# Whole-row weight pieces, a tile of its own for the last rows of v, and a conditional copy of x to DRAM

## The chip, the cores and the metric

The kernel runs on one core of one Trainium2 chip. The metric is device time in microseconds (us) of one execution, start to finish. Five engines work side by side, each in its own strict program order: PE (TensorE, matrix products), DVE (VectorE), ACT (ScalarE), POOL (GpSimd) and SP (SyncE). SP and POOL also issue most DMA transfers, and 16 DMA engines move the bytes for all of them.

## The reference

The first half is attention for 8 batches, 12 heads, 448 positions and head size 64, with an extra `exp(-m)` in the denominator. The second half is a mixture of experts over the 3584 resulting tokens of 768 numbers:

```
e   = exp(scores - m)
x   = (e / (sum(e) + exp(-m) + 1e-9)) @ v          # attention, then heads side by side: 3584 x 768
idx = argmax(cos(x, expert_emb) / tau)             # one of 8 experts for each token
out = gate * (relu(x @ w1[idx]) @ w2[idx])         # w1 768 x 1024, w2 1024 x 768 for each expert
```

With the inputs as drawn, all 448 tokens of a batch choose the same expert, in each of the 8 batches (worked out from the reference). The kernel doesn't rely on it: it runs each batch with the expert that most of its tokens chose, and a loop at the end (`other_experts`) handles the tokens that chose another one. For that loop x is kept in DRAM. With these inputs the loop has nothing to do.

## The kernel before, in words

**Tiling.** A *group* is two heads of one batch: 6 groups to a batch, 48 in all. Loads come for two groups at a time (24 loads, `n`). Of the 448 rows of q, k and v, 384 lie as 128 partitions x 3, and the last 64 rows, the *rest*, are handled apart. For a group, PE transposes q and k (`front_q`, `front_k`, L225 to L238), makes the scores in four pieces (L271, L281), ACT takes the exponential (L276), DVE subtracts 1 (L278), and PE multiplies with v (`attend`, L296, and `attend_rest`, L309). The tile `vab` holds v next to columns of ones, so that the same product also gives the denominator. POOL fills it from the loaded v (`front_v`, L249 to L257).

**Normalising.** For each two groups, the denominators go through a small DMA (`den`, L320) and DVE (`recip`, L336 to L340) to POOL, which makes the tile `rt` (L342). PE multiplies it by a selection matrix (`normalise`, L353), and DVE makes x from that (L358). Since 1 was subtracted, the sum of v over all positions is added back: POOL adds the four parts of v (`sum_v`, L194 to L196), DVE transposes and reduces it (`sum_v_rows`, L204 and L205). The tile `vs` has one buffer, so POOL's next sum can begin only when DVE's transpose has read the last one.

**Router and experts.** When a batch's six x are ready, PE, DVE and POOL find its expert (`router_mm` to `router_pick`). Then POOL issues the DMAs that fetch that expert's weights (`fetch`, L478), which also turn float32 into bfloat16. A batch's weights come in 8 pieces of 384 KB (as written): four of w1, each all 768 rows by 256 columns, and four of w2, each 256 rows by 768 columns. They share one pool of 10 buffers. `keep_xb` (L488) writes a batch's x, 672 KB, to DRAM. The expert's 15 pieces of work (`moe_chunks`: eight `h`, L495, then seven `y`, L510 and L525) are spread over six groups of later attention work.

**Order.** The work of all stages is laid out by hand in slots, 8 to a group (`pipeline`), and PE executes in just that order. For the other engines a scheduler places each instruction near its slot. A wait that is reached holds up everything behind it on that engine: a weight fetch on POOL stands in one line with `vs`, `vab` and `rt`, and on SP an output waits behind loads of q, k and v. Each `fetch` is also held behind the latest `front_v`. Outputs leave from three `y` buffers (L514 writes them on DVE, L548 and L554 issue the DMAs on SP), so the seventh `y` of a batch needs the buffer of the fourth.

**Rests of v.** `load_v` (L183 to L185) loads the main part, then the rests of all four heads into `vld` on partitions 0 to 63 (64 KB), and the rests of the odd heads a second time into the unused half of `qrest` on partitions 64 to 127 (32 KB), since `vab` needs them there (L257).

Of the kernel before, what the change touches and what calls it, by code (L numbers as in the profile page):

```python
# [9 lines left out]
F32 = mybir.dt.float32  # L10
F32R = mybir.dt.float32r
BF16 = mybir.dt.bfloat16
I32 = mybir.dt.int32
U32 = mybir.dt.uint32
ACT = mybir.ActivationFunctionType
ALU = mybir.AluOpType
# [21 lines left out]
def build_consts(k):  # L38
    nc, pool = k.nc, k.const
    k.ident = pool.tile([128, 128], F32, name="ident")  # L40
    make_identity(nc, k.ident[:])
    k.ones_f = pool.tile([128, 1], F32, name="ones_f")
    nc.vector.memset(k.ones_f[:], 1.0)
    iota_i = pool.tile([128, E], I32, name="iota_i")
    nc.gpsimd.iota(iota_i[:], pattern=[[1, E]], base=0, channel_multiplier=0)
    k.iota = pool.tile([128, E], F32, name="iota")
    nc.vector.tensor_copy(out=k.iota[:], in_=iota_i[:])

    k.vld, k.krest, k.qrest, k.vab, k.rc, k.vst = [], [], [], [], [], []
    for s in range(NG):  # L50
        v = pool.tile([128, 2 * GP, 4, DH], F32, name=f"vld{s}")
        nc.gpsimd.memset(v[64:128, :, 3, :], 0.0)
        k.vld.append(v)
        kr = pool.tile([128, GP, 128], F32, name=f"krest{s}")
        nc.vector.memset(kr[:], 0.0)
        k.krest.append(kr)
        qr = pool.tile([128, 2 * GP, DH], F32, name=f"qrest{s}")
        nc.gpsimd.memset(qr[64:128, GP:, :], 0.0)
        k.qrest.append(qr)
    for s in range(2):  # L60
        va = pool.tile([128, 4, 4, 64], F32R, name=f"vab{s}")
        for h in range(2):
            nc.vector.tensor_copy(
                out=va[:, :, 2 * h + 1, :],
                in_=k.ones_f[:, 0:1].unsqueeze(2).broadcast_to([128, 4, 64]),
            )
        k.vab.append(va)
        rc = pool.tile([128, CN], F32R, name=f"rc{s}")
        nc.vector.memset(rc[:].bitcast(F32), 0.0)
        k.rc.append(rc)  # L70
        k.vst.append(pool.tile([128, NG, 4 * GP], F32, name=f"vst{s}"))
# [50 lines left out]

def prep_expert_emb(k, emb_in, tau):
    nc = k.nc
    emb = k.wp.tile([E, DM], F32, name="emb_raw", tag="w")
    nc.sync.dma_start(emb[:], emb_in[:, :])
    sq = k.wp.tile([E, DM], F32, name="emb_sq", tag="w")
    ss = k.csp.tile([E, 1], F32, name="emb_ss", tag="cs")
    nc.scalar.activation(sq[:], emb[:], ACT.Square, accum_out=ss[:])
    nrm = k.csp.tile([E, 1], F32, name="emb_nrm", tag="cs")  # L130
    nc.gpsimd.tensor_tensor(out=nrm[:], in0=ss[:], in1=k.half[0:E, 0:1], op=ALU.pow)
    nc.vector.tensor_scalar_add(nrm[:], nrm[:], 1e-6)
    rs = k.csp.tile([E, 1], F32, name="emb_rs", tag="cs")
    nc.vector.reciprocal(out=rs[:], in_=nrm[:])
    nc.vector.tensor_scalar_mul(rs[:], rs[:], 1.0 / float(tau))
    ens = k.wp.tile([E, DM], F32, name="emb_scaled", tag="w")
    nc.vector.tensor_scalar_mul(ens[:], emb[:], rs[:])
    k.ens = ens

# [13 lines left out]
def load_qk(k, n):  # L153

    nc = k.nc
    b, h0 = n // NG, n % NG * 2 * GP
    g0, s = h0 // 2, n % NG
    t = Net()
    t.qm = k.qkp.tile([128, 3, 2 * GP, DH], F32, name="qm", tag="qm")
    t.km = k.qkp.tile([128, 3, 2 * GP, DH], F32, name="km", tag="km")  # L160
    t.kr, t.qr, t.v = k.krest[s], k.qrest[s], k.vld[s]

    def rest2(src, two):
        return src[b].rearrange("(g two) s d -> two s g d", two=2)[two, SM:S, g0 : g0 + GP, :]

    keng = nc.sync if n else nc.scalar
    for eng, dst, src in ((nc.sync, t.qm, k.q), (keng, t.km, k.k)):
        for j in range(3):
            eng.dma_start(
                dst[:, j, :, :], src[b, h0 : h0 + 2 * GP, 0:SM, :].rearrange("h (p t) d -> t p h d", t=3)[j]  # L170
            )
    nc.sync.dma_start(t.qr[0:64, :, :], k.q[b, h0 : h0 + 2 * GP, SM:S, :].rearrange("h p d -> p h d"))
    keng.dma_start(t.kr[0:64, :, 0:64], rest2(k.k, 0))
    keng.dma_start(t.kr[64:128, :, 64:128], rest2(k.k, 1))
    k.ld[n] = t


def load_v(k, n):

    nc, t = k.nc, k.ld[n]  # L180
    b, h0 = n // NG, n % NG * 2 * GP
    g0 = h0 // 2
    nc.sync.dma_start(t.v[:, :, 0:3, :], k.v[b, h0 : h0 + 2 * GP, 0:SM, :].rearrange("h (p t) d -> p h t d", t=3))  # L183
    nc.sync.dma_start(t.v[0:64, :, 3, :], k.v[b, h0 : h0 + 2 * GP, SM:S, :].rearrange("h p d -> p h d"))
    nc.sync.dma_start(  # L185
        t.qr[64:128, 0:GP, :], k.v[b].rearrange("(g two) s d -> two s g d", two=2)[1, SM:S, g0 : g0 + GP, :]
    )


def sum_v(k, n):  # L190

    nc, t = k.nc, k.ld[n]
    vs = k.vsp.tile([128, 2 * GP, DH], F32, name="vs", tag="vs")
    nc.gpsimd.tensor_tensor(out=vs[:], in0=t.v[:, :, 0, :], in1=t.v[:, :, 1, :], op=ALU.add)  # L194
    nc.gpsimd.tensor_tensor(out=vs[:], in0=vs[:], in1=t.v[:, :, 2, :], op=ALU.add)
    nc.gpsimd.tensor_tensor(out=vs[:], in0=vs[:], in1=t.v[:, :, 3, :], op=ALU.add)  # L196
    k.va[n] = vs


# [44 lines left out]
def front_v(k, g):  # L244
    nc = k.nc
    t, i = k.ld[g // GP], g % GP
    va = k.vab[g % 2]
    for h in range(2):
        nc.gpsimd.tensor_scalar(  # L249
            out=va[:, 0:3, 2 * h, :], in0=t.v[:, 2 * i + h, 0:3, :],  # L250
            scalar1=1.0, scalar2=0.0, op0=ALU.mult, op1=ALU.add,
        )
    nc.gpsimd.tensor_scalar(
        out=va[0:64, 3, 0, :], in0=t.v[0:64, 2 * i, 3, :],
        scalar1=1.0, scalar2=0.0, op0=ALU.mult, op1=ALU.add,
    )
    k.last_v = nc.gpsimd.tensor_scalar(  # L257
        out=va[64:128, 3, 2, :], in0=t.qr[64:128, i, :],
        scalar1=1.0, scalar2=0.0, op0=ALU.mult, op1=ALU.add,
    )  # L260

# [188 lines left out]
def router_pick(k, b):  # L450
# [5 lines left out]
    cnt = k.cnt_all[:, b, :]  # L456
    nc.vector.reduce_sum(out=cnt, in_=cp[:, 0 : 4 * E].rearrange("p (t e) -> p e t", e=E), axis=AX.X)
    mx = p.tile([128, 8], F32, name="mx", tag="mx")
    nc.vector.max(mx[:], cnt)
    nc.vector.max_index(k.idx_all[:, b, :], mx[:], cnt)  # L460
    idf = p.tile([128, 1], F32, name="idf", tag="idf")
# [7 lines left out]

def w_piece(k, e0, i):  # L470

    if i < 4:
        w = k.wp.tile([128, NP, F // 4], BF16, name="w", tag="w")
        src = k.w1[bass.ds(e0, 1), :, :].rearrange("o (c p) f -> p (o c) f", p=128)[:, :, F // 4 * i : F // 4 * (i + 1)]
    else:
        w = k.wp.tile([128, 2, DM], BF16, name="w", tag="w")
        src = k.w2[bass.ds(e0, 1), :, :].rearrange("o (f p) m -> p (o f) m", p=128)[:, 2 * i - 8 : 2 * i - 6, :]
    return w, k.nc.gpsimd.dma_start(w[:], src)  # L478


def fetch(k, b, i):
    w, inst = w_piece(k, k.e0[b], i)
    behind(k, inst, k.last_v)
    k.wts[b][i // 4].append(w)


def keep_xb(k, b):
    k.nc.gpsimd.dma_start(k.xb_dram[b], k.xb[b][:])  # L488


def moe_h(k, xb, w1, f):
    nc = k.nc
    ps = k.work.tile([128, 512], F32, name="work", tag="work")
    for c in range(NP):
        nc.tensor.matmul(  # L495
            ps[:, 0:S], lhsT=w1[f // 2][:, c, 128 * (f % 2) : 128 * (f % 2) + 128], rhs=xb[:, c, :],
            start=(c == 0), stop=(c == NP - 1),
        )
    h = k.hp.tile([128, S], BF16, name="h", tag="h")
    nc.scalar.activation(h[:], ps[:, 0:S], ACT.Relu)  # L500
    return h
# [57 lines left out]
def other_experts(k):  # L559
# [13 lines left out]
    with tc.If(any_ > 0):  # L573
# [6 lines left out]
        with tc.For_i(0, B * E, 1) as i:  # L580
# [3 lines left out]
            with tc.If(n > 0):  # L584
# [3 lines left out]
                g = p.tile([128, 4], F32, name="gx", tag="gx")  # L588
                nc.sync.dma_start(g[:], k.g_dram.rearrange("b e p t -> (b e) p t")[bass.ds(i, 1)].rearrange("o p t -> p (o t)"))
                nc.vector.tensor_copy(out=g[64:128, 3:4], in_=g[0:64, 3:4])  # L590
                w = [w_piece(k, e, j)[0] for j in range(8)]
                w1, w2 = w[:4], w[4:]
                hs = [moe_h(k, xb, w1, f) for f in range(NF)]
                r0 = b * S
                for t in range(3):
# [28 lines left out]
def pipeline(k):  # L624
# [37 lines left out]
    for b in range(B):  # L662
# [1 line left out]
        put(s, lambda b=b: router_mm(k, b))  # L664
        put(s + 4, lambda b=b: router_tok(k, b))
        put(s + 7.6, lambda b=b: router_pick(k, b))
        for i, o in enumerate((1, 1, 2, 3, 4, 4, 5, 6)):
            put(((b + 1) * NP + 3 + o) * NSLOT + 7.7, lambda b=b, i=i: fetch(k, b, i))
        put(s + 14, lambda b=b: keep_xb(k, b))
        put(s + 9, lambda b=b: router_exp(k, b))  # L670
# [13 lines left out]
def kernel(  # L684
# [17 lines left out]
    def pool(name, bufs, **kw):  # L702
        return ctx.enter_context(tc.tile_pool(name=name, bufs=bufs, **kw))
# [20 lines left out]
    n.xbp = pool("xbp", 3)  # L724
    n.rp = pool("rp", 1)
    n.g0p = pool("g0p", 3)
    n.wp = pool("wp", 10)
    n.hp = pool("hp", 10)
    n.yp = pool("yp", 3)
    n.ld, n.qts, n.kts, n.ems, n.nbs, n.den, n.va, n.sv = {}, {}, {}, {}, {}, {}, {}, {}  # L730
    n.lg, n.e0, n.xb, n.xs, n.ohb, n.g0, n.wts, n.avs, n.rts = {}, {}, {}, {}, {}, {}, {}, {}, {}
    n.emb, n.tau = moe_expert_emb, moe_tau
    with tc.manual_schedule(engines={mybir.EngineType.PE}):
        pipeline(n)
# [36 lines left out]
```

The softmax here doesn't subtract the row's maximum and nothing guards it: scores larger than these inputs give would overflow.

## Time and profile before

| | |
|---|---|
| median of 2 runs (lowest to highest) | 458.74 us (458.08 to 459.4) |
| profiled execution, its own time | 459.03 us |
| its span, first to last instruction | 457.2 us |
| PE busy | 406.7 us, 89% of the span |
| DVE, ACT, POOL busy | 73%, 60%, 47% |
| DMA queue of POOL (q0) | 30.68 MB written, 42.9% of 16 engines' span |
| DMA queue of SP (q1) | 44.41 MB, 41.2% |
| read from HBM, written to it | 84.17 MB, 16.52 MB |

The table reads like this. The span is shorter than the time of the execution by 1.8 us, which lies around it. A busy share is an average over the whole span: it doesn't say that an engine was the limit in a given stretch. The share of a DMA queue is the time that its packets took, divided by 16 engines times the span. The weights are read as float32 and written as bfloat16, so their bytes read are twice the bytes written.

### The profile page before, as it was taken

What the parts mean: (1) busy time and instruction counts of PE and PEld (TensorE: products, weight loads), DVE (VectorE), ACT (ScalarE), POOL (GpSimd) and SP (SyncE); (2) the same over time, 40 slices, a digit from 0 to 9 for tenths busy, and PEclk for the clock granted to TensorE, in tenths of its full rate; (3) what the DMA queues carried; (4) which work ended last, traced back from release to release, by engine and by line L of the source; (5) the groups of instructions that cost most, each with busy time, mean ns of one, the idle gap of its engine ahead of it and who ended that gap; (6) DMA issues with size and microseconds to landing.
All of it is one profiled execution on the core that took longest, in us unless ns stands there. A gap on an engine that the chain in (4) does not pass through costs nothing.

```text
span 457.2 us, 7738 instructions
## 1 busy us (share of the span) xinstructions
PE 406.7 (89%) x2392; PEld 247.1 (54%) x2392; DVE 333.0 (73%) x810; ACT 275.1 (60%) x419; POOL 213.5 (47%) x398
## 2 busy tenths in 40 slices
PE   7597779687999969988999989997999999978986
PEld 5365445454566645655466546564566655634543
DVE  4558996997699766986699777995699868853213
ACT  1557776766786646755686657765686678423120
POOL 3755454555455524733555543744554536124200
PEclk9859998988999989999999989998999999989989
DMA  9964556399969988899969999999979764973973
GB/s 175 183 154 111 127 124 176 72 167 188 218 126 201 172 210 179 149 204 199 238 119 200 182 203 191 156 215 208 204 125 199 141 139 63 202 182 72 208 166 123
DMA packets 157004, 76.25 MB, mean 167 GB/s; under 512 B 103704, under 2 KB 155928, under 8 KB 156960
## 3 DMA queue, kind: packets, MB, share of 16 engines
q0 software_dynamic: 34944, 30.68, 42.9%
q1 hardware_dynamic: 118464, 44.41, 41.2%
q10 hardware_dynamic: 3552, 0.63, 0.9%
q8 instruction: 20, 0.33, 0.3%
q14 instruction: 24, 0.20, 0.1%
HBM read 84.17 MB, written 16.52 MB: 220 GB/s over the span
## 4 chain that ended last, share of the span: by engine, by line
PE 49%; DVE 18%; DMA 11%; issue 6%; POOL 5%; ACT 4%; SPq 0%; ACTq 0%; POOLq 0%; DVEq 0%
PE work L495 12%; PE big L296 10%; DMA out_dram<-y 7%; PE work L510 6%; DVE em L278 5%; PE big L271 5%; PE work L383 4%; PE big L309 3%; DMA krest<-in_k_dram 3%; ACT e L276 3%; DVE x L358 3%; POOL rt L342 3%; PE work L353 2%; PE work L225 2%; DVE qt L228 2%
## 5 line engine op out<-in xcount | busy, mean ns | idle before, releaser
L276 ACT ACTIVATE e<-big 128x896 f32<-128x896 f32 x144 | 129.1, 921 | 40.4 <-DVE emx L285 20.5
L278 DVE TENSOR_SCALAR em<-e 128x896 fp32r<-128x896 f32 x144 | 106.8, 745 | 32.3 <-ACT e L276 31.5
L249 POOL TENSOR_SCALAR vab<-vld 128x192 fp32r<-128x192 f32 x96 | 36.3, 389 | 132.8 <-PE big L296 105.0
L495 PE MATMUL work<-xb,w 128*128 128x448 bf16 x384 | 85.3, 363 | 3.3 <-DVE y L514 2.7
L296 PE MATMUL big<-em,vab 128*128 128x448 f32 x288 | 75.6, 402 | 8.1 <-ACT e L276 7.4
L316 ACT COPY nb<-big 128x896 f32<-128x896 f32 x48 | 43.5, 907 | 49.8 <-PE big L309 49.7
L510 PE MATMUL work<-w,h 128*128 128x384 bf16 x384 | 68.7, 327 | 0.0
L358 DVE SCALAR_TENSOR_TENSOR x<-nb,sv,work 64x448 f32<-64x448 f32 x96 | 64.9, 676 | 4.1 <-PE work L353 2.3
L296 PEld LDWEIGHTS big<-em,vab 128*128 128x128 f32 x288 | 56.7, 202 | 16.0 <-ACT e L276 8.5
L514 DVE TENSOR_SCALAR y<-work,g 128x384 f32<-128x384 f32 x48 | 29.2, 609 | 41.9 <-DMA out_dram<-y 26.3
L478 POOL DMA_DIRECT2D w<-in_moe_w_dram x64 | 52.0, 816 | 15.8 <-PE work L510 5.3
L271 PE MATMUL big<-qt,kt 64*128 64x448 f32 x288 | 52.1, 412 | 7.6 <-ACT kt L240 4.1
L500 ACT ACTIVATE h<-work 128x448 bf16<-128x448 f32 x64 | 34.8, 544 | 38.8 <-PE work L495 38.6
L495 PEld LDWEIGHTS <-w 128*128 128x128 bf16 x384 | 35.9, 101 | 40.6 <-issue 16.5
L510 PEld LDWEIGHTS <-h 128*128 128x128 bf16 x384 | 35.9, 98 | 26.0 <-issue 5.4
L353 PE MATMUL work<-rt,sel 128*128 128x448 f32 x48 | 22.9, 476 | 19.9 <-DVE y L514 10.4
L228 DVE CAST qt<-work 128x448 fp32r<-128x448 f32 x48 | 29.9, 623 | 11.9 <-PE work L226 11.0
L271 PEld LDWEIGHTS big<-qt,kt 64*128 64x128 f32 x288 | 24.8, 194 | 21.9 <-issue 6.9
L240 ACT CAST kt<-work 128x512 fp32r<-128x512 f32 x48 | 28.2, 587 | 11.6 <-PE work L238 6.4
L342 POOL TENSOR_TENSOR rt<-rc,chunk 128x448 fp32r<-128x448 f32 x24 | 25.1, 1045 | 16.4 <-DVE rc L340 14.7
L194 POOL TENSOR_TENSOR vs<-vld 128x256 f32<-128x256 f32 x24 | 17.6, 735 | 28.9 <-issue 28.6
L371 ACT ACTIVATE xs<-x 128x448 f32<-128x448 f32 x48 | 27.7, 577 | 3.4 <-DVE x L358 3.4
(114 smaller groups left out, 574.2 us busy)
## 6 DMA issues: line engine op xcount, KB each, us to landing
w<-in_moe_w_dram POOLq DMA_DIRECT2D x64, 384.0 KB, 7.5
qm<-in_q_dram SPq DMA_DIRECT2D x72, 128.0 KB
vld<-in_v_dram SPq DMA_DIRECT2D x24, 384.0 KB
out_dram<-y SPq DMA_DIRECT2D x48, 192.0 KB
km<-in_k_dram SPq DMA_DIRECT2D x69, 128.0 KB
xb_dram<-xb POOLq DMA_DIRECT2D x8, 672.0 KB, 8.8
qrest<-in_q_dram SPq DMA_DIRECT2D x24, 64.0 KB
vld<-in_v_dram SPq DMA_DIRECT2D x24, 64.0 KB
```

Source lines behind the costliest of these rows:

```text
L228: nc.vector.tensor_copy(out=qt[:], in_=ps[:, 0:S])
L249: nc.gpsimd.tensor_scalar(out=va[:, 0:3, 2 * h, :], in0=t.v[:, 2 * i + h, 0:3, :], scalar1=1.0, scalar2=0.0, op0=ALU.mult, op1=ALU.add,)
L271: nc.tensor.matmul(ps[:, h, 0:S], lhsT=kt[64 * h : 64 * h + 64, 128 * j : 128 * j + 128], rhs=qt[64 * h : 64 * h + 64, :], start=True, sto ...
L276: k.last_e = nc.scalar.activation(e[:], ps[:, :, 0:S], ACT.Exp, scale=scale)
L278: k.last = nc.vector.tensor_scalar_sub(em[:], e[:], 1.0)
L296: nc.tensor.matmul(ps[:, h, 0:S], lhsT=va[:, j, 2 * h : 2 * h + 2, :], rhs=k.ems[g, j][:, h, :], start=(j == 0), stop=False,)
L316: nc.scalar.copy(out=nb[:, i, :, :], in_=ps[:, :, 0:S])
L342: nc.gpsimd.tensor_tensor(out=rt[:], in0=rc[:].bitcast(F32).unsqueeze(1).broadcast_to([128, CH, CN]), in1=k.chunk[:], op=ALU.mult)
L358: nc.vector.scalar_tensor_tensor(out=x[r, :], in0=nb[0:64, g % GP, h, :], scalar=k.sv[b][:, 2 * c + h : 2 * c + h + 1], in1=ps[r, 0:S], op ...
L478: return w, k.nc.gpsimd.dma_start(w[:], src)
L495: nc.tensor.matmul(ps[:, 0:S], lhsT=w1[f // 2][:, c, 128 * (f % 2) : 128 * (f % 2) + 128], rhs=xb[:, c, :], start=(c == 0), stop=(c == NP ...
L510: nc.tensor.matmul(ps[:, 0:SM], lhsT=hs[f][:, 128 * t : 128 * t + 128], rhs=w2[f // 2][:, f % 2, SM * n : SM * n + SM], start=(f == 0), st ...
```

## The change

There are three edits.

1. **Weights.** w1 comes in three pieces instead of four. A piece is 256 whole rows by all 1024 columns (512 KB as written) instead of all 768 rows by 256 columns. One contiguous run is now 2048 B as written instead of 512 B. Each `h` reads its six row blocks from all three pieces; before, an `h` needed one piece. w1 has 4 buffers and w2 has 5, each kind in its own, instead of 10 shared ones. The slots of the fetches follow: three for w1, four for w2 as before.
2. **Rests of v.** Two loads of 32 KB put the rests of even and odd heads on the lower and upper half of one tile `vrest`. The second copy in `qrest` goes away, `front_v` reads both halves from `vrest`, and the last addition of `sum_v` becomes two additions on 64 partitions each.
3. **x in DRAM.** `keep_xb` becomes an indirect DMA, whose 128 row numbers lie in a tile `keep_i`. Two small DVE instructions compute them: if the batch's largest count is 448, 2^20 is added, which is out of bounds, and such rows are not written.

```diff
 def load_v(k, n):
-    nc.sync.dma_start(t.v[:, :, 0:3, :], k.v[b, h0 : h0 + 2 * GP, 0:SM, :].rearrange("h (p t) d -> p h t d", t=3))
-    nc.sync.dma_start(t.v[0:64, :, 3, :], k.v[b, h0 : h0 + 2 * GP, SM:S, :].rearrange("h p d -> p h d"))
-    nc.sync.dma_start(
-        t.qr[64:128, 0:GP, :], k.v[b].rearrange("(g two) s d -> two s g d", two=2)[1, SM:S, g0 : g0 + GP, :]
-    )
+    nc.sync.dma_start(t.v[:], k.v[b, h0 : h0 + 2 * GP, 0:SM, :].rearrange("h (p t) d -> p h t d", t=3))
+    for h in range(2):
+        nc.sync.dma_start(
+            t.vr[64 * h : 64 * h + 64, :, :],
+            k.v[b].rearrange("(g two) s d -> two s g d", two=2)[h, SM:S, g0 : g0 + GP, :],
+        )
 def sum_v(k, n):
-    nc.gpsimd.tensor_tensor(out=vs[:], in0=vs[:], in1=t.v[:, :, 3, :], op=ALU.add)
+    for h in range(2):
+        r = slice(64 * h, 64 * h + 64)
+        nc.gpsimd.tensor_tensor(out=vs[r, h::2, :], in0=vs[r, h::2, :], in1=t.vr[r, :, :], op=ALU.add)
 def front_v(k, g):
-        out=va[64:128, 3, 2, :], in0=t.qr[64:128, i, :],
+        out=va[64:128, 3, 2, :], in0=t.vr[64:128, i, :],
 def w_piece(k, e0, i):
-    if i < 4:
-        w = k.wp.tile([128, NP, F // 4], BF16, name="w", tag="w")
-        src = k.w1[bass.ds(e0, 1), :, :].rearrange("o (c p) f -> p (o c) f", p=128)[:, :, F // 4 * i : F // 4 * (i + 1)]
+    if i < 3:
+        w = k.wp.tile([128, 2, F], BF16, name="w1", tag="w1")
+        src = k.w1[bass.ds(e0, 1), :, :].rearrange("o (c p) f -> p (o c) f", p=128)[:, 2 * i : 2 * i + 2, :]
     else:
-        w = k.wp.tile([128, 2, DM], BF16, name="w", tag="w")
+        w = k.wp.tile([128, 2, DM], BF16, name="w2", tag="w2", bufs=5)
 def keep_xb(k, b):
-    k.nc.gpsimd.dma_start(k.xb_dram[b], k.xb[b][:])
+    nc.vector.tensor_scalar(out=idf[:], in0=k.mx[b], scalar1=float(S), scalar2=float(1 << 20), op0=ALU.is_equal, op1=ALU.mult)
+    nc.vector.scalar_tensor_tensor(
+        out=idx[:], in0=idf[:], scalar=float(128 * b), in1=k.row[:], op0=ALU.add, op1=ALU.add
+    )
+    nc.gpsimd.indirect_dma_start(
+        out=k.xb_dram.rearrange("b p c s -> (b p) (c s)"),
+        out_offset=bass.IndirectOffsetOnAxis(ap=idx[:, 0:1], axis=0),
+        in_=k.xb[b][:].rearrange("p c s -> p (c s)"), in_offset=None,
+        bounds_check=128 * B - 1, oob_is_err=False,
+    )
 def moe_h(k, xb, w1, f):
-            ps[:, 0:S], lhsT=w1[f // 2][:, c, 128 * (f % 2) : 128 * (f % 2) + 128], rhs=xb[:, c, :],
+            ps[:, 0:S], lhsT=w1[c // 2][:, c % 2, 128 * f : 128 * f + 128], rhs=xb[:, c, :],
 def pipeline(k):
-        for i, o in enumerate((1, 1, 2, 3, 4, 4, 5, 6)):
+        for i, o in enumerate((1, 2, 3, 4, 4, 5, 6)):
```

In the program as it is built, PE's order is the same before and after. On POOL the order around a new batch changes. Before it was: fetch, fetch, the three additions of `vs`, four `vab`, fetch, `rt`. Afterwards it is: fetch, first addition, `keep_xb`, the other additions, four `vab`, fetch, `rt`. In six of the eight batches a POOL instruction right behind `keep_xb` now waits for that DMA's completion: in batches 1 to 5 the last addition of `vs` (on partitions 64 to 127), in batch 0 the last `vab` copy. Nothing in the source asks for this wait; it is in the built program's list of waits. The second w2 fetch of a batch also gets a wait for PE, for the last `y` of the batch before.

## The prediction

> **What bounds the kernel now.** I first compared one period of the pipeline with the next, cut from each batch's `rt` to the next batch's (columns: us, then busy us and instructions of PE, PEld, DVE, ACT, POOL, then granted PE clock, DMA share, GB/s).
>
> ```profile
> 126.14:177.58 51.44, 47.62 (x289) 29.34 (x288) 39.68 (x97) 33.93 (x53) 25.17 (x46) 0.97 0.94 184
> 177.58:228.31 50.73, 46.66 (x289) 28.41 (x288) 40.17 (x97) 33.70 (x53) 25.77 (x47) 1.00 0.96 188
> 228.31:279.21 50.90, 47.67 (x289) 29.24 (x288) 40.33 (x97) 34.07 (x53) 25.41 (x46) 0.97 0.97 185
> 279.21:330.03 50.82, 47.65 (x289) 29.30 (x288) 40.41 (x97) 34.03 (x53) 25.56 (x46) 0.97 0.98 188
> 330.03:376.54 46.51, 46.00 (x290) 28.47 (x289) 39.92 (x97) 34.03 (x53) 22.97 (x44) 1.00 0.83 154
> ```
>
> The same PE work takes 46.5 us when the DMA engines are 0.83 busy and 51 us when they are 0.94 to 0.98 busy. So in four periods PE loses some 4.4 us, and DMA is behind it. The chain of waits and the list of waits show where: PE waits for DVE, which waits for a `y` buffer, which waits for an output that SP could issue only after nine loads.
>
> ```profile
> PE work L353 <- DVE y L514: 10.4, 4, 3.6
> PE work L353 <- POOL rt L342: 8.9, 7, 3.2
> ```
> ```profile
> 311.17 4.44 DMA out_dram<-y
> 315.70 0.63 DVE y L514
> 316.38 0.47 PE work L353
> ```
>
> PE stood for 3.59, 1.59, 2.24 and 2.97 us at this place. After the 2.24, 2.97 and 3.59 us gaps the granted clock was halved for 3.4 us; after 1.59 us it was not. The stretch from L353 to the next L495 then took 4.66 us (316.38 to 321.04) instead of 3.22 (214.81 to 218.03): 1.4 us more. At stake here: 10.4 + 3 x 1.4 = 14.6 us.
>
> The second row is the other place where PE has no slack, L353 waiting for `rt`. I read POOL's timeline before one of them; the others look alike.
>
> ```profile
> 287.17 1.74 POOL L478 DMA_DIRECT2D w<-in_moe_w_dram  x2
> 289.85 0.74 POOL L194 TENSOR_TENSOR vs<-vld 128x256 f32<-128x256 f32 x1 [0.94 <-issue]
> 290.67 0.76 POOL L195 TENSOR_TENSOR vs<-vs,vld 128x256 f32<-128x256 f32 x1
> 291.50 1.00 POOL L196 TENSOR_TENSOR vs<-vs,vld 128x256 f32<-128x256 f32 x1
> 292.84 0.67 POOL L249 TENSOR_SCALAR vab<-vld 128x192 fp32r<-128x192 f32 x2 [0.35 <-PE big L296]
> ...
> 294.16 0.89 POOL L478 DMA_DIRECT2D w<-in_moe_w_dram  x1
> 295.12 1.03 POOL L342 TENSOR_TENSOR rt<-rc,chunk 128x448 fp32r<-128x448 f32 x1
> ```
>
> PE's L353 starts at 296.20, when `rt` ends, and PE's work before it ended at 296.08. Whatever delays POOL between 289.85 and 295.12 delays PE by as much. POOL's 47% average hides that.
>
> **Part 1, the keep DMA on POOL.** After the change this stretch holds `keep_xb` and a wait for its completion. L194 still starts at 289.85, since it waits for DVE's transpose, which ended at 289.71; so the fetch that is dropped before it saves nothing. Then: first addition to 290.65; the keep issue, 0.8 us (the plain one took 0.58, a fetch 0.80), to 291.45; second addition to 292.3; first half addition to 292.8, taken at 0.45 us, between the 0.24 of a 64x64 copy and the 0.74 of a full one. Now POOL waits. The keep DMA moves no bytes, but it stands in the same queue as the fetch issued at 287.17. Its completion lies between 2 us after its issue, the start-up of a fetch less its data (4.6 us at least, of it some 2.6 us of packets), and the 8.8 us median of the old `xb` stores, most of which also stood behind a fetch: 292.7 to 299.5.
>
> ```profile
> DMA to landing us min/median/max: 4.6/7.5/15.1
> ```
> ```profile
> DMA to landing us min/median/max: 4.4/8.8/9.8
> ```
>
> (The first row is the weight fetches, the second the stores of `xb`.) I take the fetch's median, 287.17 + 7.5 = 294.67, as the store without data ends right behind it. The last half addition ends at 295.15. In the old trace L196's end (292.50) lies 2.62 us before `rt`, 0.35 of it a wait for PE that is over by then; so `rt` starts at 295.15 + 0.1 + 2.27 = 297.5, plus 0.2 for the queue: **2.6 us late**, with ends of 0.6 and 7. A PE gap of 2.6 us lies above the 2.24 us that halved the clock; I charge half of the 1.4 us, 0.7. Six batches: 6 x 3.3 = **+19.8 us**. Queued behind the wait on POOL are four `vab`, a fetch and `rt`. `vab` has cover: it is written at 293 and first read by the attend after the next, past 306.
>
> A rule of the Trainium skill bears on the clock term. "TensorE: Matmul & The Clock Gate", "Why this matters for your kernels", asks for no idle gaps above about 3 us, one idle window; by it a 2.6 us gap would cost nothing extra, and the sum would be 4.2 us less. The trace's 2.24 us gap was followed by the half clock all the same, so I keep the charge.
>
> **Part 2, DMA work removed.** The `xb` packets took 13.5 us of all 16 engines together (1024 packets of 5376 B, 211 ns each), 1.7 a batch. The second copy of the v rests: 3072 packets of 256 B at 20.3 ns, 3.9 us in all, 0.5 a batch. w1: 24,576 packets of 512 B at 63.5 ns are 97.5 us; w2's 1536 B packets took 164 ns, so 2048 B by their slope is 214 ns, and 6144 of them are 82 us; with the packets' medians (60 and 135 ns) 66 us. That is 1.9 to 3.9 a batch. Together 4.1 to 6.1 of about 49 us.
>
> "DMA: Bandwidth & Descriptors", "Specifications", speaks against the w1 part: it calls 512 B rows enough for full rate. By that w1's packets would save nothing, and part 2 would be worth half. The two rows above give 0.124 ns a byte at 512 B and 0.107 at 1536 B, 14% apart.
>
> What reaches the path is less than what is saved. The output in question is held back in 302 to 311. There the last `xb` store is long done, and w1 is worse placed: its second piece is issued behind the late wait (297, was 288) and its third, at 302, is a third larger. The relief lies in 287 to 297, where three pieces become one; SP's loads there end sooner, but then SP waits for `yr`, which comes after the delayed L353. So I count 1.5 us a period of the 3.65 at stake, four periods: **-6 us** (bounds 0 and -14.6).
>
> **The tail.** At 384.5 six fetches were issued in a row, and the last landed at 402.2; the `den` DMA landed at 402.7, `rt` came at 403.76 and PE stood 3.19 us, then 1.4 of half clock; a last stall for `y` is 2.69. With separate buffers three pieces wait until PE's L510 is done, so `den` meets less traffic. At stake 7.3; I take **-4** (0 to -7).
>
> **Small terms.** Two DVE instructions of some 0.1 us a batch lie beside PE. The dropped memsets end at 3.6 us while POOL waits for v until 9.3: nothing. The extra half addition in POOL's first 24 us, on the chain: +0.5 (0 to 1). The second w2 fetch's wait for PE costs nothing while POOL's next copy waits for PE anyway (6.44 us at 318.19); without that cover it is some 5 us on `vab`, which has about 8. The three SP loads of v stay three, at 0.6 us each.
>
> Sum from the profiled execution: 459.03 + 19.8 - 6 - 4 + 0.5 = 469.3, so **469 us**; the median of the runs is 0.3 lower.
>
> **Rivals.** *The waits are short* (454 to 463). The keep finishes 2 us after its issue, `rt` is 0.6 to 1 us late, without clock loss: +5 with the same gains, 454; half-way, 463. For it: the queue is short when DMA has slack. Against it: fetches at this place landed after 7.1 to 8.6 us. *DMA was the whole bound* (440 to 451). The four periods fall from 51 to about 47, as the fifth did: -14.6, the tail -6, the keep +9: 447. This one is faster, and it decides where PE's stall at `y` falls below 1.6 us. For it stands the fifth period; against it that SP had no q and k loads left there, which is another thing than lighter ones. *All of w1 at the first h* (478 to 490): the third piece, issued near 304, lands after 312 at the 7.5 us median times 4/3, and the first `h` stood at 312.10; 1 to 3 us a batch more. *That x is still stored*: excluded, as L495 ran 384 = 8 x 48 times, with no other expert at work.
>
> **How the numbers follow.** The forecast (464 to 478) gets 0.44, the short waits 0.28, the DMA bound 0.20, the late w1 0.08. Two per cent, 9.2 us, is about what a measurement of this kernel can tell from no change: 449.6 to 467.9. A fifth of the forecast's chance lies below 467.9. Slower: 0.35 + 0.08 = 0.43; same: 0.28 + 0.09 = 0.37; faster 0.20. The range 447 to 481 leaves out half of the DMA case and about 0.05 above. The likeliest case's own range is 464 to 478.
>
> **What the changed profile would show.** If I am right: POOL idle 1 to 3 us inside `vs` in six batches, released by the keep DMA; PE's L353 waiting for `rt` above 20 us in all; no 5376 B packets; w1 packets near 214 ns; DMA share near 0.9 in the middle. I am wrong if that POOL wait is under 0.5 us, if the indirect issue takes several us, or if PE's wait for `y` at L353 vanishes.

## The result, and the profile after

The changed kernel takes 487.68 us (median of 2 runs, 485.81 to 489.54) against 458.74 before: 1.063 times as long, 95% interval 1.044 to 1.082. The forecast was 469 and the range ended at 481. The direction was right (slower had the largest of the three chances), the size was not: +28.9 us instead of +10. The profiled execution took 485.81 us with a span of 483.9, which is 26.7 more than the span before; that difference is taken apart here. Ratios leave out slow executions, over 1.5% longer than the fastest of the same kernel, so they aren't always the quotient of the two medians.

First the same five periods as before, from a batch's `rt` to the next batch's (us; busy us and instructions of PE, PEld, DVE, ACT, POOL; granted PE clock, DMA share, GB/s).

```profile
133.61:190.70 57.09, 49.82 (x289) 30.35 (x288) 39.19 (x99) 33.81 (x53) 25.40 (x49) 0.91 0.74 152
190.70:247.97 57.27, 50.28 (x289) 30.56 (x288) 40.03 (x99) 33.82 (x53) 25.50 (x48) 0.91 0.75 152
247.97:302.15 54.18, 48.12 (x289) 29.08 (x288) 40.22 (x99) 33.74 (x53) 26.12 (x49) 0.97 0.81 162
302.15:354.35 52.20, 47.52 (x289) 28.96 (x288) 38.93 (x99) 33.80 (x53) 25.39 (x49) 0.97 0.78 161
354.35:407.78 53.43, 48.53 (x289) 29.68 (x288) 39.27 (x99) 33.82 (x53) 23.09 (x45) 0.94 0.62 120
```

In the first four, the DMA share lay between 0.94 and 0.98 before and lies between 0.74 and 0.81 now, and yet the periods are longer: the DMA share doesn't rise with the time here. Cut into its three parts, `rt` to `rt`, a period shows where. These are the second period before and the second after.

```profile
177.58:193.49 15.91, 15.82 (x99) 10.40 (x98) 14.74 (x47) 12.92 (x22) 10.44 (x19) 1.00 0.81 135
193.49:209.82 16.33, 14.85 (x97) 9.47 (x96) 13.57 (x29) 9.76 (x15) 7.07 (x14) 1.00 1.05 196
209.82:228.31 18.49, 16.00 (x97) 8.53 (x96) 11.86 (x22) 11.02 (x19) 8.25 (x15) 1.00 1.01 228
```
```profile
190.70:210.82 20.12, 16.70 (x102) 10.75 (x100) 16.34 (x52) 13.87 (x23) 10.94 (x19) 1.00 0.62 119
210.82:228.46 17.64, 16.57 (x92) 10.45 (x93) 11.96 (x25) 8.81 (x13) 7.20 (x16) 0.81 0.76 144
228.46:247.97 19.51, 17.01 (x97) 9.36 (x96) 11.73 (x22) 11.14 (x19) 7.36 (x14) 0.91 0.88 194
```

The first part grew by 4.2 us at full clock: PE stands. The second grew at a clock of 0.81: PE runs slowly after having stood. Over all five periods the first parts grew by 21.0 us (79.9 to 100.9), the second by 9.0 (76.7 to 85.8), and the third parts shrank by 6.3 (93.8 to 87.5). Besides that, the stretch up to the fourth `rt` (start-up) grew by 2.1, batch 0 (fourth to seventh `rt`) by 5.4, and the tail behind the last of these periods shrank by 4.5. The sum is 26.7.

POOL's timeline in the first part, with the wait in brackets, and PE's beside it:

```profile
198.63 0.79 POOL L485 DMA_DIRECT2D w<-in_moe_w_dram  x1
201.06 0.73 POOL L198 TENSOR_TENSOR vs<-vld 128x256 f32<-128x256 f32 x1 [1.64 <-issue]
201.98 1.07 POOL L503 DMA_INDIRECT xb_dram<-xb,keep_i  x1 [0.19 <-issue]
203.07 1.06 POOL L199 TENSOR_TENSOR vs<-vs,vld 128x256 f32<-128x256 f32 x1
204.22 0.72 POOL L202 TENSOR_TENSOR vs<-vs,vrest 64x128 f32<-64x128 f32 x1
208.08 0.45 POOL L202 TENSOR_TENSOR vs<-vs,vrest 64x128 f32<-64x128 f32 x1 [3.14 <-DMA xb_dram<-xb,keep_i]
...
210.82 1.02 POOL L348 TENSOR_TENSOR rt<-rc,chunk 128x448 fp32r<-128x448 f32 x1
```
```profile
207.06 0.50 PE L287 MATMUL work<-qt,kt 128*128 128x448 f32 x1
211.89 0.74 PE L359 MATMUL work<-rt,sel 128*128 128x448 f32 x1 [4.34 <-POOL rt L348]
```

The wait is where the prediction put it, and PE stands 4.34 us for `rt`. The keep DMA landed 6.03 us after its issue at 201.98, so at 208.01. The weight fetch that was issued ahead of it at 198.63 had taken

```profile
DMA to landing us min/median/max: 8.1/8.1/8.1
```

and so landed at 206.8, 1.2 us before the keep. In batches 0 to 5 the fetch ahead took 6.4 to 8.8 us (median 8.1), and the keep landed 0.8 to 2.6 us behind it. In sum, from the lists of waits of PE and of POOL, and the keep DMA's time from issue to landing:

```profile
PE work L359 <- POOL rt L348: 30.2, 11, 4.7
PE work L359 <- DVE y L534: 5.6, 3, 2.5
```
```profile
POOL vs L202 <- DMA xb_dram<-xb,keep_i: 15.4, 5, 3.3
```
```profile
DMA to landing us min/median/max: 2.4/6.0/6.2
```

### The profile page after: what moved, and what is told of

It is laid out like the page before. It is cut to its first block, busy times and chain, and to the rows that moved or that the text cites. A ratio compares the mean times of both kernels' runs of the same rounds, so it can differ in the third digit from the quotient of the medians.

```text
span 483.9 us, 7759 instructions
## 1 busy us (share of the span) xinstructions
PE 416.8 (86%) x2392; PEld 253.3 (52%) x2392; DVE 328.4 (68%) x827; ACT 274.5 (57%) x419; POOL 213.6 (44%) x412
## 4 chain that ended last, share of the span: by engine, by line
PE 44%; DVE 16%; POOL 14%; issue 12%; DMA 6%; ACT 2%; POOLq 0%; SPq 0%; DVEq 0%; ACTq 0%
PE big L302 9%; PE work L515 8%; PE work L530 5%; DVE x L364 5%; DMA out_dram<-y 5%; PE big L277 5%; PE work L389 4%; DVE em L284 3%; PE work L545 3%; PE work L359 3%; POOL rt L348 3%; PE big L315 2%; POOL vs L202 2%; POOL vs L199 2%; PE work L231 2%
## 5 line engine op out<-in xcount | busy, mean ns | idle before, releaser
L284 DVE TENSOR_SCALAR em<-e 128x896 fp32r<-128x896 f32 x144 | 97.9, 680 | 39.0 <-ACT e L282 37.4
L255 POOL TENSOR_SCALAR vab<-vld 128x192 fp32r<-128x192 f32 x96 | 34.7, 374 | 139.2 <-PE big L302 109.9
L515 PE MATMUL work<-xb,w 128*128 128x448 bf16 x384 | 83.1, 356 | 3.7 <-DVE y L534 1.6
L302 PE MATMUL big<-em,vab 128*128 128x448 f32 x288 | 77.4, 409 | 6.5 <-ACT e L282 5.5
L322 ACT COPY nb<-big 128x896 f32<-128x896 f32 x48 | 43.5, 907 | 61.0 <-PE big L315 60.9
L302 PEld LDWEIGHTS big<-em,vab 128*128 128x128 f32 x288 | 59.0, 210 | 15.3 <-ACT e L282 7.5
L277 PE MATMUL big<-qt,kt 64*128 64x448 f32 x288 | 55.0, 434 | 5.4 <-ACT kt L246 2.4
L359 PE MATMUL work<-rt,sel 128*128 128x448 f32 x48 | 25.7, 535 | 38.7 <-POOL rt L348 30.2
L485 POOL DMA_DIRECT2D w<-in_moe_w_dram x56 | 43.4, 779 | 13.7 <-PE work L530 5.8
L359 PEld LDWEIGHTS work<-rt,sel 128*128 128x128 f32 x48 | 10.3, 214 | 49.2 <-POOL rt L348 35.9
L202 POOL TENSOR_TENSOR vs<-vs,vrest 64x128 f32<-64x128 f32 x48 | 26.6, 554 | 18.5 <-DMA xb_dram<-xb,keep_i 15.4
```

The source lines that it names most:

```text
L202: nc.gpsimd.tensor_tensor(out=vs[r, h::2, :], in0=vs[r, h::2, :], in1=t.vr[r, :, :], op=ALU.add)
L277: nc.tensor.matmul(ps[:, h, 0:S], lhsT=kt[64 * h : 64 * h + 64, 128 * j : 128 * j + 128], rhs=qt[64 * h : 64 * h + 64, :], start=True, sto ...
L284: k.last = nc.vector.tensor_scalar_sub(em[:], e[:], 1.0)
L302: nc.tensor.matmul(ps[:, h, 0:S], lhsT=va[:, j, 2 * h : 2 * h + 2, :], rhs=k.ems[g, j][:, h, :], start=(j == 0), stop=False,)
L322: nc.scalar.copy(out=nb[:, i, :, :], in_=ps[:, :, 0:S])
L359: nc.tensor.matmul(ps[:, 0:S], lhsT=k.sel[:, g % GP, :], rhs=rt[:].rearrange("p c n -> p (c n)"), start=True, stop=True)
```

## The experiments

Every kernel was timed beside the kernel before on the same chip; the median of the kernel before was 460.12 us beside E1 to E4, 462.62 beside E5 to E8, 459.62 beside E9 to E12 and 459.65 beside E13 to E15. Ratios are to those runs. The changed kernel was not timed again beside them, so a difference to its 487.68 us is uncertain by the 4 us by which the kernel before varied (458.74 to 462.62).

### E1 to E3: the wait moved away, the DMA taken out, the plain store put back

E1 is the changed kernel with the same indirect DMA behind `rt`:

```diff
-    nc.gpsimd.indirect_dma_start(
+    inst = nc.gpsimd.indirect_dma_start(
...
+    behind(k, inst, k.last_rt)
-        put(s + 14, lambda b=b: keep_xb(k, b))
+        put(s + 17, lambda b=b: keep_xb(k, b))
```

> The changed kernel with the same indirect keep DMA, but issued behind the batch's first rt instead of ahead of it. In the built program the wait for its completion then falls on the next group's last vab copy, where POOL waits some 6 us for PE anyway. Theory A (the wait's place costs the time: 4.2 us of late rt and 0.8 to 2.7 us of half clock in each of five batches, some 5 us in batch 0): rt is no longer late, PE's wait for rt at L361 falls from 30.2 us to under 10, and the time falls by 25 to 35 us, to 451 to 462. Rival B (the indirect form itself costs, through its issue of 1.07 us or through traffic, wherever it stands): 475 or more. Rival C (the gap at rt only moves to the wait for y once rt is in time): 465 to 475.

E2 drops the write of x altogether, E3 has the old store:

```diff
 def keep_xb(k, b):
+    pass
```

> The changed kernel without any write of x to DRAM: the keep DMA and its two DVE instructions are left out (the loop over other experts would read nothing useful; it has nothing to do with these inputs). Theory A: the same as with the keep behind rt, within 3 us, 448 to 462, since that one's keep has cover. Rival B (the indirect DMA costs wherever it stands): 8 us or more below the run with the late keep.

```diff
 def keep_xb(k, b):
+    k.nc.gpsimd.dma_start(k.xb_dram[b], k.xb[b][:])
```

> The changed kernel with the old plain store of x (672 KB a batch) in place of the indirect one; whole-row weights and the vrest tile stay. No POOL instruction waits for it in the built program. Theory A: the bytes are cheap and the wait was dear: 1 to 6 us above the run without a keep, 452 to 464, faster than the changed kernel by 24 us or more. Rival (the removed bytes were worth as much as the wait cost): above 470.

Measured: E1 462.21 us (ratio 1.006, 1.000 to 1.012), E2 457.25 (1.001, 0.997 to 1.006), E3 455.18 (0.994, 0.989 to 0.999). All three are 25 to 33 us below the changed kernel. E1 keeps the indirect DMA and moves only its place, and that takes back 25.5 us of the 28.9 that were lost; without a wait for the store (E2, E3) it is 30.4 and 32.5. So the place of one wait, which no line of the source asks for, is worth nearly the whole loss. In E1 PE's wait for `rt` fell from 30.2 to 6.1 us, as theory A said. The time came out 0.2 us above the range that it gave. PE's wait for `y` was 21.7 us in its profiled execution (464.49, above its median), and the third parts of its periods sum to 107.2 us (87.5 in the changed kernel): so part of what was won at `rt` was lost at `y`, as rival C had it. E11 below takes that loss away. Whether the late keep costs a few us against no keep (E1 against E2) isn't told apart by intervals that overlap. E3 against E2 shows that the 672 KB a batch were cheap: the kernel that writes them is no slower than the one that doesn't.

E2 has no wait, no bytes of x and light weight packets. If lighter DMA relieved PE's wait for `y`, it would show here. PE's list of waits has

```profile
PE work L359 <- DVE y L521: 10.6, 4, 3.0
```

where it was 10.4 before, and its five periods take 250.3 us, against 250.4 before, with a DMA share of 0.83 to 0.87 in the four long ones. SP's timeline of E2 shows where the output stands (the one that is waited for is at 212.85):

```profile
204.72 2.20 SPq L172 DMA_DIRECT2D qm<-in_q_dram  x3
207.01 3.64 SPq L172 DMA_DIRECT2D km<-in_k_dram  x3
210.70 0.66 SPq L175 DMA_DIRECT2D qrest<-in_q_dram  x1
211.46 0.65 SPq L176 DMA_DIRECT2D krest<-in_k_dram  x1
212.15 0.60 SPq L177 DMA_DIRECT2D krest<-in_k_dram  x1
212.85 1.01 SPq L555 DMA_DIRECT2D out_dram<-y  x2
```

The output stands behind the same nine loads in SP's order, and these take 8.1 us to issue; before, it was 8.9 (302.22 to 311.17).

### E4 and E7: edit 1 alone, edit 3 alone

E4 is the kernel before with edit 1 of the diff, E7 with edit 3, both as shown under the change.

> The kernel before with edit 1 alone (w1 in three pieces of whole rows, buffers of their own). My forecast's terms: the tail -4 and part of the -6 at y, since w1's packets are 1 to 2 us of DMA time a batch fewer: 449 to 456 against 458.7. Rival (packets save nothing, 512 B rows were enough): 457 to 460. Rival (all of w1 needed at the first h): 462 or more, with PE waiting for w1 at L495 or for the h behind it.

> The kernel before with edit 3 alone: indirect keep, four w1 pieces and the old rests of v. In the built program the same wait for the keep falls on the fourth vab copy, which also stands ahead of rt. If the wait is the cost and needs neither of the other edits: rt is late by 3 to 5 us in six batches with the half clock after it, 480 to 495. If the wait matters only behind the half additions on vrest: 457 to 465.

E4: 452.86 us (0.989, 0.977 to 1.002), within the forecast, though the interval doesn't exclude no change. The rows below are the stretch behind the last full period, before and in E4, cut at the last `rt`:

```profile
376.54:403.76 27.22, 24.94 (x152) 15.30 (x150) 21.67 (x62) 15.48 (x25) 10.02 (x15) 1.00 0.84 138
403.76:457.20 53.44, 44.42 (x255) 22.44 (x255) 16.66 (x49) 10.38 (x20) 10.27 (x13) 0.94 0.71 147
```
```profile
377.24:401.41 24.17, 24.00 (x147) 14.92 (x146) 21.22 (x62) 15.49 (x25) 8.16 (x13) 1.00 0.71 133
401.41:451.80 50.39, 42.44 (x262) 21.76 (x259) 16.70 (x49) 10.46 (x20) 9.80 (x13) 0.98 0.76 167
```

The tail is 6.1 us shorter, while the five periods (253.1 us) are no shorter than before (250.4) and PE's wait for `y` is 11.8 us. Before, six fetches were issued in a row from 384.5; in E4 four from 385.2, and the next three at 402.4, behind the last `rt`. The last `den` DMA, issued at 397.32 before and at 398.06 in E4, was thus followed by `rt` after 3.4 us instead of 6.4.

E7: 488.34 us (1.055, 1.046 to 1.064), as slow as the whole change. Here the wait falls on a `vab` copy instead of on `vs`, so the other edits aren't needed for it. PE's list of waits, the keep's time to landing with two fetches ahead of it instead of one, and a row of POOL's list of waits:

```profile
PE work L357 <- POOL rt L346: 41.2, 11, 6.1
```
```profile
DMA to landing us min/median/max: 2.2/8.0/8.7
```
```profile
POOL vab L261 <- DMA qrest<-in_q_dram: 17.6, 4, 4.9
```

The last row names loads of `qrest`, but the copy follows the keep in the trace: in batches 0 to 3 it starts 0.23 to 0.25 us after the keep has landed (97.97 after 97.72, 149.53 after 149.29, 204.03 after 203.80). The five first parts are 28.1 us longer than before, and PE's wait for `y` at L357 is gone, with the old w1 packets: the third parts sum to 77.9 us, against 93.8 before.

### E6: the queue ahead of the keep emptied

The first weight fetch of a batch goes behind `rt`; the keep and the wait on `vs` stay:

```diff
 def fetch(k, b, i):
     behind(k, inst, k.last_v)
+    if i == 0:
+        behind(k, inst, k.last_rt)
-            put(((b + 1) * NP + 3 + o) * NSLOT + 7.7, lambda b=b, i=i: fetch(k, b, i))
+            put(((b + 1) * NP + 3 + o) * NSLOT + (7.7 if i else 8.9), lambda b=b, i=i: fetch(k, b, i))
```

> The changed kernel with the first w1 fetch of a batch issued behind rt, so that nothing stands in POOL's DMA queue when the keep DMA is issued; the wait for the keep stays on the same vs addition. Theory A (the keep's 6.0 us are the fetch ahead of it): it lands after 2.4 to 3.5 us, POOL's wait for it falls from 3.3 to under 0.7 us, rt is late by under 1 us, and the time is 457 to 467. Rival (an indirect DMA of 128 rows takes 5 to 6 us by itself): landing and wait stay, 480 or more.

Measured: 477.13 us (1.032, 1.024 to 1.041), between the two theories. The landing and POOL's wait, as its list of waits has it, were

```profile
DMA to landing us min/median/max: 2.3/3.7/4.1
```
```profile
POOL vs L202 <- DMA xb_dram<-xb,keep_i: 1.3, 1, 1.3
```

The list names the keep for one batch only. For others it names PE, but the addition starts just after the keep has landed there too (202.39 in this one):

```profile
202.46 0.45 POOL L202 TENSOR_TENSOR vs<-vs,vrest 64x128 f32<-64x128 f32 x1 [0.92 <-PE work L243]
```

In batches 1 to 5 POOL waited 0.3 to 1.3 us in this way, 4.6 in all, where the changed kernel has 15.4. Theory A was right in its direction, but it had put the landing at 2.4 to 3.5 us and the wait under 0.7.

So an indirect DMA whose rows all lie out of bounds lands after a median of 3.7 us alone, 6.0 behind one fetch and 8.0 behind two. The total missed for two more reasons. The first parts of the five periods are still 1.3 us longer than before on average. And part of the gain was lost elsewhere: the first and second parts sum to 161.6 us (before 156.6, after the change 186.7), but the third parts to 105.1 (93.8, 87.5), with PE waiting 18.4 us for `y`, and the tail takes 82.1 (80.7, 76.1). That is a profiled execution of 483.43, above its own median, so these losses may be smaller in the others.

### E5 and E10: the gaps filled

32 small products (128x256, unused) stand in PE's order ahead of the L359 that waits:

```diff
+    for b in range(6):
+        put((b + 1) * NP * NSLOT + 46.4, lambda: warm(k, 32))
```

> The changed kernel with 32 small PE products (128x256, result unused) ahead of each first L359 of a batch, for batches 0 to 5, where PE stood 4.2 to 4.7 us. They take 3.5 us at full clock. If the half clock after the gap is its own cost (second parts of the periods 17.5, 17.6, 16.5, 16.5, 17.6 us after against 14.9 to 16.3 before): the first parts stay at 20 us, the second parts fall to 15 to 15.9, and 5 to 9 us go, 477 to 482 against 487.7; some of it can come back as a longer wait for y in the third parts. If the longer second parts have another cause: no change, 485 to 489.

> The changed kernel with 32 small PE products in each gap at rt, once more, one look: first parts near 20.2, second parts near 15.1, third parts 20 to 23 us, as in the run before; 485 to 490.

Measured: 487.42 us (1.057, 1.050 to 1.065), and 487.36 in E10, one execution of the same kernel. The total says no change. The parts say something else: the second parts fell to 15.0, 15.7, 15.0, 15.5 and 15.0 us, 9.7 less in sum, and the loss came back at `y`, where the third parts grew from 87.5 to 102.6:

```profile
PE work L359 <- DVE y L534: 15.6, 4, 5.2
```

against 5.6 without the filling. The wait at `rt` and the wait at `y` hide one another: PE that comes later to `y` finds the output further on.

### E8, E12 and E14: the wait for y taken away

Six `y` buffers instead of three (`n.yp = pool("yp", 6)`): E8 with edit 1 alone, E12 with the kernel before, E14 as E8 without the write of x (`keep_xb` does nothing).

> The kernel before with edit 1 and six y buffers in place of three. The runs with less DMA traffic left PE's wait for y at L353 at 10.6 to 11.8 us. If that wait is for the buffer, and so for the place of the output in SP's queue: it falls under 2 us, the half clock behind it goes too, and the time falls by 8 to 15 us from 452.9, to 438 to 445. If DMA itself is the bound (the output or the loads only arrive later elsewhere): 450 to 455, with a new wait of PE for loads or weights.

> The kernel before with six y buffers alone. If the whole-row weights are worth the tail only (some 5 us, as the stretch behind the last full period showed: 80.7 us before, 74.6 with edit 1): 439 to 442. If they also help the middle once y no longer bounds it: 443 or more. If they are worth nothing: 433 to 437.

> Edit 1 with six y buffers, and x not written to DRAM at all (the loop over other experts would read nothing useful; it has nothing to do here). If the 672 KB a batch are hidden: 433 to 436, as the 434.7 with the store. If those bytes cost once y no longer bounds it: 431 or less.

Measured: E8 434.66 us (0.943, 0.936 to 0.951), E12 440.49 (0.959, 0.952 to 0.966), E14 433.02 (0.941, 0.936 to 0.946). E8 is the fastest kernel here that still stores x; it is faster than the kernel before and the changed one, and by more than was forecast. Two of its periods, and one of E12's:

```profile
219.11:265.56 46.45, 45.94 (x289) 28.36 (x288) 39.69 (x97) 33.93 (x53) 24.51 (x46) 1.00 0.98 207
265.56:311.99 46.43, 45.88 (x289) 28.38 (x288) 39.27 (x97) 33.80 (x53) 24.50 (x45) 1.00 0.96 202
```
```profile
220.33:266.50 46.17, 45.93 (x289) 28.36 (x288) 40.12 (x97) 33.93 (x53) 25.15 (x46) 1.00 1.05 204
```

46.4 us with the DMA engines 0.96 to 0.98 busy, and in E12, with the same DMA work as before, 46.2 us at a share of 1.05 (the packets' times divided by 16 engines times the stretch, which can pass 1): what the prediction read from the five periods before, that a full DMA makes 51 us out of 46.5, was wrong. Three buffers instead of six made it. E12's periods take 233.7 us, E8's 232.5, so the light packets still give nothing in the middle; E8's advantage is the tail (73.1 us, E12's 81.7). E14 shows that the bytes of x are worth nothing that can be told from the runs here either.

### E9 and E13: the price of the wait, with nowhere to go

The changed kernel with six `y` buffers, E13 with the gaps filled as in E5.

> The changed kernel with six y buffers, so that PE no longer waits for y and the loss at rt stands alone. Reference: edit 1 with six y buffers ran in 434.7 us. If the losses are 4.2 us of late rt and 0.8 to 2.7 us of half clock in five batches, some 5 us in batch 0 and 3 us in the start-up: 434.7 + 30 + 5 + 3 = 473, range 466 to 480. If the changed kernel's shorter third parts (19.5, 19.5, 17.7, 15.4 us) came from less DMA traffic and not from the delay: the gain by six buffers is under 8 us, 480 or more.

> The changed kernel with six y buffers and the gaps at rt filled with 32 small PE products. With three buffers the filled gaps moved the loss to y and the time stayed at 487.4. With six buffers nothing can move there: if the half clock is a loss of its own, the second parts fall from 15.4 to 18.0 us to about 15, and the time falls by 8 to 12 us from 474.2, to 462 to 466. If it isn't: 472 to 476.

Measured: E9 474.15 us (1.032, 1.022 to 1.043), E13 465.67 (1.013, 1.006 to 1.019). One period of each:

```profile
186.18:206.90 20.72, 16.68 (x102) 10.75 (x100) 16.29 (x52) 13.89 (x23) 11.01 (x20) 1.00 0.63 123
206.90:224.58 17.68, 16.61 (x92) 10.46 (x93) 11.95 (x25) 8.83 (x13) 7.21 (x16) 0.81 0.74 143
224.58:239.95 15.37, 15.27 (x97) 8.54 (x96) 11.44 (x22) 11.11 (x19) 7.18 (x15) 1.00 1.07 236
```
```profile
183.00:203.88 20.88, 19.73 (x130) 13.55 (x129) 16.46 (x53) 13.89 (x23) 11.38 (x20) 1.00 0.66 126
203.88:220.28 16.40, 15.67 (x103) 9.87 (x100) 11.36 (x24) 9.62 (x14) 7.34 (x15) 1.00 0.82 168
```

The third part is back at 15.4 us. E9's five periods take 264.3 us. Those of E11 (below), which differs from E9 only in the place of the keep, take 235.6: the wait costs 5.7 us a batch when nothing hides it (6.4 against E8's 232.5, which has neither edit 2 nor 3). The filled gaps leave the first part as it is and give the second part full clock; 8.5 us go from the median, and the second parts' sum falls by as much, from 85.7 to 77.2 (in the profiled executions batch 0 gave 3.8 more, and the start-up lost 2.7). So the halved clock is a loss of its own, some 1.7 us for each gap, beside the 3.6 to 4.5 us by which E9's first parts are longer than E8's.

### E11 and E15: the late keep without the wait for y, and the start-up

E11 is E1 with six `y` buffers. E15 adds an order on DVE: `prep_expert_emb` later, and its `emb_nrm` and `emb_scaled` behind the `qt` copy placed before them.

> The changed kernel with the keep behind rt and six y buffers. With three buffers it lost 21.7 us at y against 10.6 without a keep. If all of that is the buffer: 434.7 + 3 for the start-up, 436 to 441. If the late keep or its 1152 small packets cost by themselves: 445 or more.

> The changed kernel with the keep behind rt and six y buffers (441.9 us), and the scaling of the expert embeddings on DVE moved behind later work, so that DVE's qt copy near 41 us no longer stands behind it. If that order cost the start-up its 2.4 us gap and the half clock after it: rt of the first group comes at 38.5 to 39.5, the time falls by 2 to 4 us, to 438 to 440. If not: 441 to 443.

Measured: E11 441.89 us (0.965, 0.957 to 0.972), E15 441.49 (0.963, 0.957 to 0.969). E11 lies 0.9 us above the range of its first theory and 7 us above E8; of the profiled executions 2.0 lie ahead of the seventh `rt`, 3.1 in the five periods and 2.6 in the tail. So the late keep or edit 2 still cost a little, and it isn't settled which.

The start-up of the changed kernel, DVE and then PE:

```profile
39.77 0.14 DVE L135 TENSOR_SCALAR emb_nrm<-emb_nrm 8x1 f32<-8x1 f32 x1 [1.19 <-POOL emb_nrm L134]
39.95 0.18 DVE L346 TENSOR_TENSOR rc<-den,rc 56x32 fp32r<-56x32 f32 x1
...
40.53 1.19 DVE L140 TENSOR_SCALAR emb_scaled<-emb_raw,emb_rs 8x768 f32<-8x768 f32 x1
41.65 0.60 DVE L234 CAST qt<-work 128x448 fp32r<-128x448 f32 x1
```
```profile
42.40 0.44 PE L359 MATMUL work<-rt,sel 128*128 128x448 f32 x1 [2.36 <-DVE qt L234]
```

Before, DVE made `rc` (38.22) and copied `qt` (38.48) ahead of `emb_nrm`; now `rc`, from which POOL makes `rt`, stands behind `emb_nrm`, which waits for POOL, and the copy stands behind four instructions on the embeddings. The first two `rt` come at 40.28 and 55.78 (38.60 and 52.61 before). E3, with edits 1 and 2, has 40.29 and 55.80; E4, with edit 1 alone, 38.43 and 52.45; E7, with edit 3 alone, 38.29 and 52.31. So edit 2 brings it. That it does so through DVE's order is read from the timelines, not shown by a run, for E15's cure failed: the first `rt` came at 39.44, but then PE had to wait for the scaling,

```profile
PE work L150 <- DVE emb_scaled L140: 6.0, 1, 6.0
```

and the time stayed.

## Why the prediction was wrong

The sum failed at its first term, the keep's wait: +19.8 us were forecast and 35.4 measured (30.0 in the five periods, 5.4 in batch 0). The other terms came near their numbers, one of them by luck: -6.3 at `y` (-6 forecast), -4.5 in the tail (-4), +2.1 in the start-up (+0.5); together 26.7.

**The wait of POOL for the keep (+19.8): right mechanism, too small.** POOL's wait sat where it was said, behind `vs`, and took 15.4 us in five batches. It was put at 3.3 us a batch for the gap and the clock together; the five periods lost 6.0 each. The first step to fail was the landing: "as the store without data ends right behind it", the keep was taken to land with the fetch, a median fetch's 7.5 us after that one's issue; it landed 9.4 us after it (198.63 to 208.01). Of this the fetch took 8.1. The 7.5 was the median of all 64 fetches; those at this place had taken 7.4 to 8.9 us before (the prediction gives 7.1 to 8.6), and the new one is a third larger. The keep then landed 1.2 us behind it, not at the same time. So `rt` came 4.2 us late, not 2.6. The range of this term (0.6 to 7 us) held 4.2; the sum took the wrong value in it. The Trainium skill, "DMA: Bandwidth & Descriptors", "SWDGE vs HWDGE vs iDMA", says that of the queues that POOL's DMAs go through only one is allocated; 3.7, 6.0 and 8.0 us behind none, one and two fetches agree with it.

**The clock charge (0.7 a gap): too small.** With gaps of 4.2 to 4.7 us the halved stretch lasted 3.4 or 6.8 us, and E13 against E9 prices it at 1.7 us where nothing hides it. The charge was half of the 1.4 us seen after shorter gaps. To charge gaps under 3 us at all went against the rule of the Trainium skill, "TensorE: Matmul & The Clock Gate", "Why this matters for your kernels" (no idle gaps above about 3 us); the runs show both cases. PE stood 2.36 us at 40.03, and from 43.5 to 50.4 the clock was at 0.52; but in E2 gaps of 3.00 and 2.69 us (at 163.68 and 266.67) were followed by the full clock.

**The relief at `y` (-6): right number, wrong reason.** The third parts did shrink by 6.3 us. But lighter DMA did not do it: in E2, with all of the bytes saved and no wait, and in E4 the wait for `y` stayed at 10.6 and 11.8 us. In the changed kernel PE was late at `rt`, so the output was further on when PE came to need its buffer; E5 made PE earlier and the wait grew back from 5.6 to 15.6 us, and E9 without the wait for `y` has third parts of 15.4. That the number fits is luck. What failed here is the opening of the prediction: "DMA is behind it". A DMA share of 0.94 to 0.98 stood beside the long periods; E12 runs them in 46.2 to 47.4 us at 1.00 to 1.05, E8 in 46.4 to 46.6 at 0.91 to 0.98. The wait is for one of three buffers, as E8 and E12 show; that the output comes late because it stands behind nine loads on SP, which the prediction named too, is read from the timelines, and no run moved it there.

**The tail (-4): right.** -4.5 in the changed kernel, -6.1 in E4, for the reason given: three pieces wait until PE is done with the last expert, `den` is sooner done, and the last `rt` keeps PE waiting 1.28 us (0.11 in E4) instead of 3.19. The last of the six fetches before landed at 402.8, not at 402.2. Whether the separate buffers do this or the longer rows was not tried apart.

**The start-up (+0.5): too small, and for another reason.** +2.1 up to the fourth `rt`. The step asked only for POOL's extra addition; in the trace it is DVE's order that changed. The prediction follows PE's and POOL's order in the built program and says nothing of DVE's.

**The packets of w1: right, and without effect in the middle.** 2048 B took 203 ns where 214 was forecast, and the w1 packets cost 78.0 us of 16 engines instead of 97.5. (The upper 3.9 us a batch sets a sum of means, 97.5, against one of medians, 66; with medians on both sides, 92.2 and 66, it is 3.2.) None of it reached the middle of the kernel. The DMA share there fell to 0.74 to 0.81, where the prediction expected near 0.9.

**The rivals.** *Short waits* (454 to 463) fell with the 9.4 us. *DMA was the whole bound* fell with E2, E8 and E12. *All of w1 at the first h*: PE waited for a weight once, for 1.6 us. The range ended at 481 because it took the upper end of no term: 4.2 us and 1.7 us in six batches alone make +35, less the 10 that were counted back, so some 484.

## What to carry to other kernels

When an edit changes the kind of a DMA, look in the built program for waits it brings along, and price such a wait by what is ahead of the DMA in its queue, at that place, and by a landing of its own behind it, not by its bytes; here moving it behind the instruction on the path took 25 us back. A resource that is busy while PE waits is not yet the cause: take the wait away by another means (a buffer) and see whether the resource stays as busy, as it did here at 0.98 and more. And a loss at one wait can hide another wait further on, so that two losses can't be added or removed one at a time; and an edit can move the order of an engine that it doesn't name.

## What the runs showed of the hardware that was not expected

An indirect DMA whose rows are all out of bounds isn't free. Its issue took POOL 1.07 us (a weight fetch 0.79), and it still sends packets. The rows of POOL's queue, of the changed kernel and of E2 without the keep:

```profile
q0 software_dynamic: 16384, 25.17, 32.6%
```
```profile
q0 software_dynamic: 15232, 25.17, 34.7%
```

The same bytes, but 1152 packets more: 8 keeps of 144, which are one for each of the 128 rows and the 16 that every fetch has too (896 for E2's 56 fetches). All of them are packets of 4 B in the trace.

After PE gaps of 4.2 to 4.7 us the granted clock was halved for either one or two stretches of 3.4 us, and which of the two varied between gaps of nearly one length: 6.8 us after 4.34 (at 207.55), 3.4 us after 4.21 (at 264.83). In the ten gaps at a batch's first `rt` in the five periods of the changed kernel and of E9, it went with the moment at which the clock fell. Where PE worked again before the fall or at most 0.04 us after it, the stretch was 3.4 us (269.04 and a fall at 269.00; five gaps). Where PE came 0.25 to 1.75 us after the fall, it was 6.8 (211.89 and 210.98; five gaps). It isn't a strict rule: in E10, after a wait for `y`, PE came 0.6 us after a fall (175.65 and 175.08), and the stretch was 3.4 us.

Why the framework adds the wait for an indirect DMA was not found; the experiments only moved it. In the traces of the changed kernel, E1, E6, E7 and E9 it falls on the next POOL instruction that works on partitions 64 to 127 alone.
